# Squared-relu attention and MLP: score tiles leave PSUM through VectorE's relu, with the square on ScalarE

## The chip, the core and the metric

The kernel runs on one core of a Trainium2 chip. A core has TensorE (matrix products into PSUM), VectorE, ScalarE, GpSimd and the DMA queues. The metric is device time in microseconds of one execution.

## What is computed

Attention with a squared relu instead of a softmax, and behind it an MLP with a squared relu:

```python
scores = scale * np.matmul(q, k.transpose(0, 1, 3, 2))   # (8, 12, 448, 448)
attn = np.maximum(scores, 0.0) ** 2 / S                  # S = 448
attn_out = np.matmul(attn, v)                            # (8, 12, 448, 64)
x = attn_out.transpose(0, 2, 1, 3).reshape(3584, 768)
h = x @ w_in                                             # (3584, 2048)
r = np.maximum(h, 0.0)
out = (r * r) @ w_out                                    # (3584, 768), float32
```

All inputs are float32; the kernel multiplies in float16 and sums in float32.

## The kernel before, in words

The eight batches of 12 heads are cut into 24 units of four heads (`n`), three a batch. A unit has seven rounds (`t`), one for each group of 64 keys. `scores` (line 281) makes one round: four small matmuls with 64x64 weights write to a PSUM tile `sp` of two banks (pool `s_p`, two buffers), 128 partitions by 896 columns for one round with all 448 queries. `soft` (line 288) turns it into the float16 tile `at`, and `av` (line 316) multiplies that with V into two `avt` tiles of the PSUM pool `mm_p` (four buffers). At the end of a unit, or of two, copies bring `avt` to SBUF as `xt` (line 329 on ScalarE, line 331 on VectorE). `h_group` makes the hidden layer from `xt` (line 179), squares its relu with `relu2`, and `o_groups` (line 219) makes the output tiles, copied out by ScalarE (line 227) and stored by SP's queue.

There are two ways from scores to `at`. `relu2` (lines 158, 159): ScalarE squares from PSUM, then VectorE masks the square with (score > 0), reading PSUM again. `relu2_wide` (lines 166, 167): ScalarE's relu goes to a float32 tile `rel` in SBUF (pool `rel_p`, four buffers, shared with the output tiles), and VectorE or GpSimd multiplies it by itself.

Batch 0 is written out by hand: in it all five engines take their instructions in program order. Its queries are done in two parts, 256 and 192 wide (`PARTS`), with two rounds in a PSUM tile, so there are 22 tiles `i`, 11 (`NA`) for each part, of 1024 and of 768 columns; tiles 10 and 21 hold one round. In each turn of the loop TensorE makes the scores of tile `i`, then the A·V products of an older tile (`put(i - 2)` in the first part, `put(i - 3)` in the second), in the second part one hidden half-group (`some_h`, six matmuls), and what stands in `beside`: transposes of later units (`turn_pe`, with a copy out of PSUM on VectorE or ScalarE, line 105), loads, casts (line 89). Tiles 5, 8, 12, 15 and 18 are multiplied by GpSimd (`engs`), the others by VectorE. Ahead of the loop GpSimd's queue holds the casts of units 1 and 2, loads of V, and the loads of the first weights (line 127).

Then the main loop runs over pairs of rounds. A turn makes the scores of two rounds, perhaps all A·V products of an older unit in one burst, then `soft` for both, then loads and casts (`upkeep`), and then so much of the queued hidden and output work as keeps the backlog even (`run_some`). In this part only TensorE and SP follow program order; a planner with a cost model orders the instructions of VectorE, ScalarE and GpSimd. In the rest of batch 1 (`n < 2 * NU`) the second tile of a pair goes by `relu2_wide` with GpSimd, all others by `relu2`.

Of the kernel before, what the change touches and what calls it, by code (L numbers as in the profile page):

```python
# [11 lines left out]
AF = mybir.ActivationFunctionType  # L12
# [4 lines left out]
def kernel(  # L17
# [9 lines left out]
    nc = tc.nc  # L27

    B, H, S, D = q.shape
# [8 lines left out]
    NU = 3  # L38
# [5 lines left out]
    SK = 256.0  # L44
# [29 lines left out]
    def load_qk(n, w, eng, gate=None):  # L74
        b, u = divmod(n, NU)
        t = raw_p.tile([P, 2, TJ * D], FP32, name=w + "f", tag=w + "f")
        if gate is not None:
            gate.memset(t[0:1, 0, 0:1], 0.0)
        src = q if w == "q" else k
        eng.dma_start(  # L80
            out=t,
            in_=src[b, 4 * u:4 * u + 4].rearrange(
                "(f e) (p t) d -> (e p) f (t d)", e=2, t=TJ))
        raw[n, w] = t
# [23 lines left out]
    def load_v(b, us):  # L108

        if b not in vst:  # L110
            vst[b] = v_p.tile([P, NU, 2, TJ * D], FP16, name="vs", tag="vs")
        src = v[b].rearrange("(u x) (p t) d -> p u x (t d)", x=4, t=TJ)
        for r in range(2):
            rows = slice(64 * r, 64 * r + 64)
            hs = slice(1, 3) if r else slice(0, 4, 3)
            if isinstance(us, int):
                nc.gpsimd.dma_start(out=vst[b][rows, us], in_=src[:, us, hs])
            else:
                for i, h in enumerate(range(4)[hs]):
                    nc.gpsimd.dma_start(out=vst[b][rows, :, i], in_=src[:, :, h])  # L120
# [36 lines left out]
    def relu2(ps, dst, scale):  # L157
        nc.scalar.activation(out=dst, in_=ps, func=AF.Square, scale=scale)  # L158
        nc.vector.scalar_tensor_tensor(  # L159
            out=dst, in0=ps, scalar=0.0, in1=dst, op0=ALU.is_gt, op1=ALU.mult)  # L160

    def relu2_wide(ps, dst, scale, eng):

        r = rel_p.tile([P, 2, 512], FP32, name="rel", tag="wide")
        r = r[:, :, 0:ps.shape[-1]]
        nc.scalar.activation(out=r, in_=ps, func=AF.Relu, scale=scale)  # L166
        eng.tensor_mul(dst, r, r)  # L167

    def h_group(b, fs, cols):
        pr = b // 2  # L170
# [114 lines left out]
                    skip_group_check=True)  # L285
        return sp

    def soft(sp, width, eng=None):
        at = at_p.tile([P, 2, 512], FP16, name="at", tag="at")
        at = at[:, :, 0:width]  # L290
        if eng is None:
            relu2(sp[:, :, 0:width], at, SK)
        else:
            relu2_wide(sp[:, :, 0:width], at, SK, eng)
        return at

    avs_open: dict = {}

    def av(n, t, cols=WHOLE, copy=None):

        b, u = divmod(n, NU)
        if b not in xts:
            xts[b] = x_p.tile([P, NM, S], FP16, name="xt", tag="xt")
        w = cols.stop - cols.start
        vs = vst[b]
        at0 = w if w < S and u == 1 else 0
        if t == 0:
            avs_open[n] = avs_open[n - 1] if at0 else [
                mm_p.tile([P, 512], FP32, name="avt", tag="mm") for _ in range(2)]
        ap = avs_open[n]  # L310
        at = ats.pop((n, t))
        for e in range(2):
            for c in range(2):
                f = c ^ e
                r = slice(64 * c, 64 * c + 64)
                nc.tensor.matmul(  # L316
                    ap[f][64 * e:64 * e + 64, at0:at0 + w],
                    lhsT=vs[r, u, e ^ c, t * D:(t + 1) * D],
                    rhs=at[r, e, :],
                    start=(t == 0), stop=(t == TJ - 1), skip_group_check=True)  # L320
        if t < TJ - 1 or (w < S and u == 0):
            return
        for f in range(2):
            dst, src = xts[b][:, 2 * u + f, cols], ap[f][:, 0:w]
            if at0:
                dst = xts[b][:, f:f + 3:2, cols]
                src = ap[f][:, 0:2 * w].rearrange("p (u c) -> p u c", c=w)
            if copy is None:
                nc.scalar.activation(out=dst, in_=src, func=AF.Copy, scale=CX)  # L329
            else:  # L330
                copy.tensor_scalar_mul(dst, src, CX)  # L331
# [41 lines left out]
    with tc.manual_schedule():  # L373
        load_qk(0, "k", nc.sync)
        load_qk(0, "q", nc.scalar)
        for n in (1, 2):
            load_qk(n, "k", nc.sync)
            load_qk(n, "q", nc.sync)
        idle = const_p.tile([P, 512], FP16, name="idle", tag="idle")
        nc.vector.memset(idle, 0.0)  # L380
        ident = const_p.tile([P, P], FP16, name="ident", tag="ident")
        make_identity(nc, ident)
        load_v(0, 0)

        warm = mm_p.tile([P, 512], FP32, name="warm", tag="mm")
        for _ in range(12):
            nc.tensor.matmul(warm, lhsT=idle[:, 0:P], rhs=idle, start=True, stop=True)  # L387
        cast_qk(0, "k", dve)
        cast_qk(0, "q", act)
        turn_pe(0, "k", dve)  # L390
        turn_pe(0, "q", dve)
        cast_qk(1, "k", pool)
        load_v(0, 1)
        cast_qk(1, "q", pool)
        load_v(0, 2)
        cast_qk(2, "k", pool)
        load_w1(0)
        cast_qk(2, "q", pool)
        load_w1(1)
        for w in "kq":  # L400
            load_qk(3, w, nc.sync, nc.gpsimd)
        load_w1(2)
        load_w1(3)

        rounds = [divmod(r, TJ) for r in range(STREAM)]
        tiles = [(part, rounds[r:r + 2]) for part in range(2) for r in range(0, STREAM, 2)]
        NA = len(tiles) // 2
        engs = {z: nc.vector for z in range(2 * NA)}
        engs.update({z: nc.gpsimd for z in (5, 8, NA + 1, NA + 4, NA + 7)})
        beside = {  # L410
            1: [(turn_pe, 1, "k", dve)],
            2: [(turn_pe, 1, "q", dve)],
            3: [(turn_pe, 2, "k", dve)],
            4: [(turn_pe, 2, "q", dve)],
            8: [(load_qk, 4, w, nc.sync, nc.gpsimd) for w in "kq"],
            NA + 1: [(cast_qk, 3, "k", pool), (cast_qk, 3, "q", pool)],
            NA + 4: [(load_v, 1, slice(None)), (load_w2, 0, 0), (load_w2, 0, 1)],
            NA + 6: [(turn_pe, 3, "k", dve)],
            NA + 7: [(load_qk, 5, w, nc.sync, nc.gpsimd) for w in "kq"]
            + [(load_w2, 1, 0), (load_w2, 1, 1)],  # L420
            NA + 8: [(turn_pe, 3, "q", act)],
        }
        first_h = deque(z for f in range(0, NF, 2) for z in h_group(0, [f, f + 1], PARTS[0]))
        made: dict = {}

        def put(i):
            part, rs = tiles[i]
            for n, t in rs:
                ats[n, t] = made.pop((part, n, t))
                av(n, t, PARTS[part], nc.vector if part else None)  # L430

        def some_h():
            for _ in range(NM):
                first_h.popleft()[1]()

        for i, (part, rs) in enumerate(tiles):
            cols = PARTS[part]
            w = cols.stop - cols.start
            sp = None
            for j, (n, t) in enumerate(rs):  # L440
                sp = scores(n, t, sp, j * w, cols)
            at = soft(sp, len(rs) * w, engs.get(i))
            for j, (n, t) in enumerate(rs):
                made[part, n, t] = at[:, :, j * w:(j + 1) * w]
            if 2 <= i < NA + 2:
                put(i - 2)
            if i >= NA + 3:
                put(i - 3)
            if i > NA + 1:
                some_h()  # L450
            for fn, *a in beside.get(i, ()):
                fn(*a)
        for i in range(len(tiles) - 3, len(tiles)):
            put(i)
            some_h()
# [3 lines left out]
    for i in range(STREAM // 2, NB):  # L459
        g = []  # L460
        for r in range(max(STREAM, 2 * i), 2 * i + 2):
            n, t = divmod(r, TJ)
            g.append((n, t, scores(n, t)))
        if i in avs:
            for t in range(TJ):
                av(avs[i], t)
        for z, (n, t, sp) in enumerate(g):
            ats[n, t] = soft(sp, S, nc.gpsimd if n < 2 * NU and z == 1 else None)
        if i in pushes:
            push_dense(pushes[i])  # L470
        upkeep(i)
        nxt = min([j for j in pushes if j > i] or [NB + 2])
        run_some(max(0.0, (queued - KEEP) / (nxt - i)))
# [37 lines left out]
```

## Time and profile before

| | |
|---|---|
| median of 8 runs | 418.41 us (417.4 to 418.85) |
| the profiled execution | 417.56 us, its span 415.6 us |
| TensorE busy | 396.3 us, 95% |
| VectorE busy | 246.4 us, 59% |
| ScalarE busy | 257.5 us, 62% |
| GpSimd busy | 98.2 us, 24% |
| VectorE's squares in batch 0 (L167) | 17, 22.8 us |
| ScalarE's relus (L166) | 32, 28.1 us |
| VectorE's masks of scores (L159) | 137, 143.7 us |

In the profile PE is TensorE, PEld its weight loads, DVE VectorE, ACT ScalarE, POOL GpSimd, and SP the queue that issues most DMAs. Times are us from the start of the span. Brackets at the end of a timeline row give the idle time before it and what ended it. `x8` is the number of instructions merged in a row. L167 is line 167. The granted clock of TensorE is given as a fraction of full speed.

### The profile page before, as it was taken

Reading aid. Unit: us, or ns where it says so; the run is one execution under the profiler, and the core shown is the slowest. Engines: PE = TensorE matmul, PEld = TensorE weight load, DVE = VectorE, ACT = ScalarE, POOL = GpSimd, SP = SyncE. Lnnn points to the kernel's source line nnn. Section 1 sums busy time; section 2 is a strip of 40 time slices with the busy share of each in tenths; the row PEclk is TensorE's granted clock in tenths of the full one; section 3 lists DMA queues with packets and bytes.
Section 4 is the critical chain, followed back from the end, with each engine's and each line's share of the span. In section 5 each row is a group of like instructions: output and inputs, shape, how many; then the busy total and the mean of one; then the engine's idle time right before and its main releaser. Section 6 shows DMA issues by size and latency. Waiting matters only on the chain.

```text
span 415.6 us, 8125 instructions
## 1 busy us (share of the span) xinstructions
PE 396.3 (95%) x3368; PEld 211.6 (51%) x3368; DVE 246.4 (59%) x297; ACT 257.5 (62%) x404; POOL 98.2 (24%) x115
## 2 busy tenths in 40 slices
PE   7668899999999999999999999999999999999995
PEld 3445476544445444544455444544455445555562
DVE  2868685369875686486664686486664686142200
ACT  3476398778876676676666676676766676243211
POOL 5559677752302201210112301210100000000000
PEclk9669899999999999999999999999999999999998
DMA  8999999879509933790918833690614010201122
GB/s 278 180 236 177 231 269 184 212 173 294 133 2 159 252 79 94 123 197 17 240 45 158 250 80 93 123 198 18 154 39 95 26 39 0 55 25 38 39 76 76
DMA packets 65445, 53.61 MB, mean 129 GB/s; under 512 B 35841, under 2 KB 62209, under 8 KB 65409
## 3 DMA queue, kind: packets, MB, share of 16 engines
q1 hardware_dynamic: 51152, 40.84, 38.9%
q0 software_dynamic: 13984, 11.80, 19.1%
q8 instruction: 26, 0.43, 0.4%
q10 hardware_dynamic: 272, 0.46, 0.3%
q14 instruction: 11, 0.08, 0.1%
HBM read 45.61 MB, written 11.01 MB: 136 GB/s over the span
## 4 chain that ended last, share of the span: by engine, by line
PE 92%; DVE 4%; ACT 2%; issue 1%; POOL 0%; ACTq 0%; DVEq 0%
PE hps L179 36%; PE ops L219 36%; PE sp L281 10%; PE avt L316 8%; DVE at L167 2%; ACT rel L166 1%; PE tps L103 1%; PE warm L387 1%; DVE at L159 0%; POOL at L167 0%; DVE g L159 0%; DVE kT L105 0%; DVE qT L105 0%; ACT at L158 0%; ACT xt L329 0%
## 5 line engine op out<-in xcount | busy, mean ns | idle before, releaser
L159 DVE SCALAR_TENSOR_TENSOR at<-sp,at 128x896 f16<-128x896 f32 x137 | 143.7, 1086 | 81.1 <-ACT at L158 80.8
L179 PE MATMUL hps<-xt,w 128*128 128x448 f16 (+2 forms) x864 | 159.2, 335 | 0.0
L158 ACT ACTIVATE at<-sp 128x896 f16<-128x896 f32 x137 | 118.9, 915 | 62.0 <-PE sp L281 62.0
L219 PE MATMUL ops<-w,g 128*128 128x384 f16 x896 | 157.1, 326 | 0.0
L219 PEld LDWEIGHTS <-g 128*128 128x128 f16 x896 | 84.3, 98 | 67.9 <-issue 14.2
L179 PEld LDWEIGHTS <-w 128*128 128x128 f16 x864 | 80.3, 99 | 69.2 <-issue 11.5
L159 DVE SCALAR_TENSOR_TENSOR g<-hps,g 128x448 f16<-128x448 f32 (+2 forms) x128 | 76.1, 619 | 46.1 <-ACT g L158 45.7
L158 ACT ACTIVATE g<-hps 128x448 f16<-128x448 f32 (+2 forms) x128 | 68.0, 551 | 31.9 <-PE hps L179 31.0
L281 PE MATMUL sp<-qT,kT 64*64 64x448 f16 (+2 forms) x756 | 53.5, 352 | 5.1 <-DVE qT L105 4.0
L89 POOL CAST ks<-kf 128x896 f16<-128x896 f32 x23 | 22.7, 985 | 127.9 <-DMA kf<-in_k_dram 126.8
L227 ACT ACTIVATE osb<-ops 128x384 f32<-128x384 f32 x56 | 27.8, 496 | 38.4 <-PE ops L219 32.7
L316 PE MATMUL avt<-at,vs 64*64 64x448 f16 (+2 forms) x756 | 42.7, 343 | 6.2 <-DVE xt L331 2.0
L166 ACT ACTIVATE rel<-sp 128x1024 f32<-128x1024 f32 (+4 forms) x32 | 28.1, 895 | 13.6 <-PE sp L281 13.6
L281 PEld LDWEIGHTS <-kT 64*64 64x64 f16 x756 | 17.4, 108 | 33.5 <-issue 30.4
L316 PEld LDWEIGHTS <-vs 64*64 64x64 f16 x756 | 23.5, 111 | 19.4 <-issue 9.9
L120 POOL DMA_DIRECT2D vs<-in_v_dram x28 | 17.5, 633 | 50.9 <-PE avt L316 50.9
L167 POOL TENSOR_TENSOR at<-rel 128x896 f16<-128x896 f32 (+2 forms) x15 | 25.2, 1680 | 13.6 <-ACT rel L166 13.5
L167 DVE TENSOR_TENSOR at<-rel 128x1024 f16<-128x1024 f32 (+3 forms) x17 | 22.8, 1355 | 8.0 <-ACT rel L166 7.9
L329 ACT ACTIVATE xt<-avt 128x448 f16<-128x448 f32 (+2 forms) x46 | 22.4, 549 | 3.0 <-PE avt L316 2.9
L89 POOL CAST qs<-qf 128x896 f16<-128x896 f32 x23 | 22.3, 969 | 6.5 <-DMA qf<-in_q_dram 6.4
L387 PE MATMUL warm<-idle 128*128 128x512 f16 x12 | 5.3, 632 | 1.2 <-DVE idle L380 1.2
L103 PE MATMUL tps<-ident,ks 128*128 128x128 f16 x42 | 4.1, 251 | 1.6 <-DVE g L159 1.6
(23 smaller groups left out, 36.6 us busy)
## 6 DMA issues: line engine op xcount, KB each, us to landing
kf<-in_k_dram SPq DMA_DIRECT2D x24, 448.0 KB, 4.6
qf<-in_q_dram SPq DMA_DIRECT2D x23, 448.0 KB, 5.3
out_dram<-osb SPq DMA_DIRECT2D x50, 192.0 KB, 2.7
vs<-in_v_dram POOLq DMA_DIRECT2D x28, 168.0 KB, 5.5
w<-in_moe_w_in_dram POOLq DMA_DIRECT2D x4, 768.0 KB, 14.7
w<-in_moe_w_out_dram POOLq DMA_DIRECT2D x4, 768.0 KB, 20.3
out_dram<-osb SPq DMA_DIRECT2D x12, 96.0 KB, 2.9
vs<-in_v_dram POOLq DMA_DIRECT2D x6, 112.0 KB, 4.0
```

Source lines behind the costliest of these rows:

```text
L89: op(t.rearrange("p t (f d) -> p f t d", f=2), src.rearrange("p f (t d) -> p f t d", d=D))
L120: nc.gpsimd.dma_start(out=vst[b][rows, :, i], in_=src[:, :, h])
L158: nc.scalar.activation(out=dst, in_=ps, func=AF.Square, scale=scale)
L159: nc.vector.scalar_tensor_tensor(out=dst, in0=ps, scalar=0.0, in1=dst, op0=ALU.is_gt, op1=ALU.mult)
L166: nc.scalar.activation(out=r, in_=ps, func=AF.Relu, scale=scale)
L167: eng.tensor_mul(dst, r, r)
L179: nc.tensor.matmul(cell[0][:, i * w:i * w + w], lhsT=w1[f // 4][:, m, (f % 4) * P:(f % 4 + 1) * P], rhs=xts[b][:, m, cols], start=(m == 0) ...
L219: nc.tensor.matmul(cell[0][:, 0:HALF], lhsT=gt[f][:, tb * P:(tb + 1) * P], rhs=w2[hf][f // 8][:, f % 8, :], start=(f == 0), stop=(f == NF ...
L227: nc.scalar.activation(out=cell[1][:, at:at + HALF], in_=cell[0][:, 0:HALF], func=AF.Copy, scale=CO)
L281: nc.tensor.matmul(sp[64 * c:64 * c + 64, e, at:at + w].rearrange("p (t c) -> p t c", c=TP), lhsT=kT[r, t, 64 * e:64 * e + 64], rhs=qT[r, ...
L316: nc.tensor.matmul(ap[f][64 * e:64 * e + 64, at0:at0 + w], lhsT=vs[r, u, e ^ c, t * D:(t + 1) * D], rhs=at[r, e, :], start=(t == 0), stop= ...
L329: nc.scalar.activation(out=dst, in_=src, func=AF.Copy, scale=CX)
```

## The change

A tile can now take its first step on VectorE: the relu out of PSUM, to float32 in SBUF. ScalarE then squares it from SBUF with the scale. The other form, ScalarE's relu and GpSimd's square, stays for some tiles; the form with a multiplication on VectorE is no longer used. In batch 0 tile 2 joins tiles 5, 8, 12, 15 and 18 on ScalarE and GpSimd; the other 16 go VectorE, then ScalarE. There the second step of a vector tile is held back (`seconds`): it is issued in the next turn of the loop, behind the next tile's first step if that is ScalarE's. In the main loop the first tile of each pair goes VectorE, then ScalarE, to the end; the second goes ScalarE, then GpSimd, in batch 1, and by `relu2` after it. Both first steps are issued ahead of both second steps.

```diff
-    def relu2_wide(ps, dst, scale, eng):
+    def by_sbuf(ps, dst, scale, first):
 
         r = rel_p.tile([P, 2, 512], FP32, name="rel", tag="wide")
         r = r[:, :, 0:ps.shape[-1]]
+        if first is nc.vector:
+            nc.vector.tensor_scalar_max(r, ps, 0.0)
+            return lambda: nc.scalar.activation(out=dst, in_=r, func=AF.Square, scale=scale)
         nc.scalar.activation(out=r, in_=ps, func=AF.Relu, scale=scale)
-        eng.tensor_mul(dst, r, r)
+        return lambda: nc.gpsimd.tensor_mul(dst, r, r)
...
-    def soft(sp, width, eng=None):
+    def soft(sp, width, first=None):
...
-        if eng is None:
+        if first is None:
             relu2(sp[:, :, 0:width], at, SK)
-        else:
-            relu2_wide(sp[:, :, 0:width], at, SK, eng)
-        return at
+            return at, None
+        return at, by_sbuf(sp[:, :, 0:width], at, SK, first)
...
-        engs = {z: nc.vector for z in range(2 * NA)}
-        engs.update({z: nc.gpsimd for z in (5, 8, NA + 1, NA + 4, NA + 7)})
+        firsts = {z: nc.scalar for z in (2, 5, 8, NA + 1, NA + 4, NA + 7)}
...
+        seconds: list = []
...
-            at = soft(sp, len(rs) * w, engs.get(i))
+            first = firsts.get(i, nc.vector)
+            if first is nc.vector and seconds:
+                seconds.pop()()
+            at, second = soft(sp, len(rs) * w, first)
+            if seconds:
+                seconds.pop()()
+            if first is nc.vector:
+                seconds.append(second)
+            else:
+                second()
...
+        seconds.pop()()
         for i in range(len(tiles) - 3, len(tiles)):
             put(i)
             some_h()
...
+        todo = []
         for z, (n, t, sp) in enumerate(g):
-            ats[n, t] = soft(sp, S, nc.gpsimd if n < 2 * NU and z == 1 else None)
+            first = nc.vector if z == 0 else nc.scalar if n < 2 * NU else None
+            ats[n, t], second = soft(sp, S, first)
+            todo.append(second)
+        for second in filter(None, todo):
+            second()
```

## The prediction, made blind

> **What bounds the kernel now.** I read the page first, then the busy time by stretches, then the timeline of the first 60 us. By stretches (us, busy and count of each engine, granted clock, DMA share, GB/s):
>
> ```profile
> 12.00:15.50 3.50, 0.43 (x8) 0.24 (x6) 3.50 (x4) 0.00 (x0) 3.50 (x7) 0.78 0.89 111
> 15.50:20.20 4.70, 4.64 (x66) 3.26 (x66) 3.01 (x5) 2.48 (x3) 0.88 (x2) 0.50 1.17 205
> ...
> 42.60:44.65 2.05, 0.02 (x1) 0.00 (x0) 1.77 (x3) 1.05 (x3) 2.05 (x3) 1.00 1.15 157
> 44.65:48.30 3.65, 3.65 (x31) 1.89 (x34) 1.56 (x3) 0.00 (x0) 1.15 (x2) 0.53 1.18 238
> ...
> 50.30:66.00 15.70, 15.67 (x201) 12.10 (x201) 12.13 (x16) 14.55 (x22) 12.41 (x13) 1.00 1.22 254
> 66.00:90.00 24.00, 23.32 (x231) 12.56 (x228) 11.35 (x13) 18.44 (x29) 17.77 (x16) 1.00 0.92 190
> 90.00:385.00 295.00, 295.00 (x2314) 148.99 (x2311) 189.04 (x231) 192.77 (x309) 36.10 (x44) 1.00 0.48 109
> ```
>
> From 90 to 385 us TensorE is busy all the time at full clock; VectorE and ScalarE are at 64% and 65%. Nothing this change does there can gain. TensorE idles 14 us in the first 90, nearly all of it before 50.3, where batch 0 ends and the saturated part begins; a us won there is a us at the end. Two of the idle spells (3.1 us up to 15.5, 2.05 up to 44.65) are followed by half clock. The timeline shows who was late:
>
> ```profile
> 14.74 1.64 POOL L127 DMA_DIRECT2D w<-in_moe_w_in_dram  x2
> 14.90 0.61 DVE L105 COPY qT<-tps 128x896 f16<-128x896 f16 x1
> 15.56 0.43 PE L281 MATMUL sp<-qT,kT 64*64 64x256 f16 x4 [3.13 <-DVE qT L105]
> ...
> 34.57 2.17 DVE L167 TENSOR_TENSOR at<-rel 128x768 f16<-128x768 f32 x1 [0.26 <-ACT rel L166]
> ...
> 37.27 0.94 DVE L167 TENSOR_TENSOR at<-rel 128x768 f16<-128x768 f32 x1
> 37.40 0.55 PE L103 MATMUL tps<-ident,ks 128*128 128x128 f16 x7 [1.64 <-DVE g L159]
> ...
> 44.05 1.01 DVE L331 TENSOR_SCALAR xt<-avt 128x384 f16<-128x384 f32 x2
> 44.65 0.53 PE L316 MATMUL avt<-at,vs 64*64 64x192 f16 x7 [2.03 <-DVE xt L331]
> ```
>
> Each time TensorE waits for a small VectorE step that stands in the queue behind squares. The same square of 768 columns takes 0.94 us alone and 2.17 beside GpSimd's square and DMA issue.
>
> **Prices of the new operations.** The groups of instructions with shapes kept apart (count, busy us, mean ns, idle before):
>
> ```profile
> L166 ACT ACTIVATE rel<-sp 128x896 f32<-128x896 f32 x10 | 9.1, 913 | 0.0
> ...
> L331 DVE TENSOR_SCALAR xt<-avt 128x384 f16<-128x384 f32 x2 | 1.0, 544 | 0.0
> ...
> L89 ACT CAST qs<-qf 128x896 f16<-128x896 f32 x1 | 0.9, 938 | 2.8 <-DMA qf<-in_q_dram 2.8
> ...
> L331 DVE TENSOR_SCALAR xt<-avt 128x192 f16<-128x192 f32 x2 | 0.6, 353 | 0.0
> ```
>
> VectorE's relu is a one-input operation out of PSUM like L331: 0.995 ns a column and 162 ns fixed, so 1.18 us at 1024 columns, 1.05 at 896, 0.93 at 768. The other end is the mask L159, 1086 ns at 896, so 1.21 at 1024; I take L331, the same kind of operation. ScalarE's square out of SBUF is priced by the cast of line 89: 938 against 913 ns, 25 ns more than out of PSUM: 1.05 at 1024, 0.84 at 768. GpSimd's square has its own row (1.89 at 20.87 us, 1.46 at 768). [...]
>
> **Batch 0.** Before, 17 tiles cost VectorE a square (22.8 us, mean 1.35 with the disturbed ones). Now 16 cost it a relu (7 x 1.18, 7 x 0.93, two short ones: 15.9 us). ScalarE trades 16 relus for 16 squares (+0.4 us). Tile 2 joins the GpSimd tiles. I walk the four queues in program order, each step starting when its engine is free and its inputs are there (0.04 us for a handover).
>
> Start: scores of tile 0 end at 8.93. Relus of tiles 0 and 1 on VectorE last to 11.35, ScalarE's square of tile 0 ends at 11.2, so the first A·V starts as before (11.29). The q copy, which waited behind three squares, now follows its transposes at 12.2 and is done at 12.8 rather than 15.5. That stall goes.
>
> What is late next is tile 2. GpSimd's queue, with the casts and weight loads ahead of it, is busy to 14.74 + 1.64 = 16.38; its square ends at 18.3. Nothing queues behind it on GpSimd until tile 5, but TensorE, in order, does: the A·V of tile 2 comes at 18.35 (17.85 before); TensorE idles from 14.2. The whole gain of the start is lost here, with 0.5 us on top.
>
> Tiles 3 to 12: a vector tile's square queues on ScalarE behind the next scalar tile's relu. Scores of 5 end at 20.3 (18.35 + A·V 0.43 + transposes 0.86 + scores 0.6), relu 5 to 21.3, square 4 to 22.3; GpSimd's square of 5 ends at 23.3, the A·V of 5 starts there (22.81 before). Then ScalarE: relu 8 to 25.5, square 7 +1.0, two copies +1.1, squares 9 and 10 +1.6, which is 29.2; relu 12 from 29.7 to 30.5, square 11 to 31.3, two copies to 32.0. The first hidden group needs those: it ends at 32.2, before at 30.75. So 1.4 us late.
>
> Tiles 13 to 21: VectorE's six squares from 31.04 on took 2.67 + 2.17 + 0.94 + 2.00 + 1.25 = 9.0 us; six relus take 5.6. Of these 3.4 us I lose 0.7 to waits for ScalarE, which has squares and the hidden groups' squares in one queue. The copies at 44.05 come at 42.8 (1.4 - 3.4 + 0.7), and the A·V behind them at 43.4 in place of 44.65. TensorE then idles 0.4 us there, not 2.05, so I expect the half clock of 44.65:48.30 to go: from the A·V to the last hidden group 3.9 us, not 5.7. End of batch 0 at 47.4, not 50.35: -3.0. The same walk of the old kernel gives 49.9, 0.4 early, so I book -2.6.
>
> **After batch 0.** Until 90 us GpSimd keeps the second tile of a turn, and the first goes VectorE, then ScalarE. Both PSUM tiles are free after about 1.1 us instead of 2.0 and 1.8; the one such wait in the trace, 0.6 us at 84.6, goes: -0.5. The new wait: ScalarE's square stands behind VectorE's relu, which can stand behind a mask (0.68), and behind the square queue the hidden groups' squares, for which TensorE waits. At least 0, if those are placed first. At most six turns of (1.05 - 0.91 + 0.68) = 4.9 us, less ScalarE's idle time of 1.15 in 50.3:66, less 2.2 that TensorE can run ahead (two PSUM buffers of 12 matmuls; 21 took about 2.0 us): 1.6. With ScalarE at 93% there I take +1.1. From 90 us on each pair costs ScalarE 25 ns more and VectorE 30 less, hidden by the third of each that is idle; uncovered it would be 1.6 us over 63 turns. The relu buffers, four, are now shared with output tiles to the end: 0 to +1, I take 0.
>
> Sum: -2.6 - 0.5 + 1.1 = -2.0. The profiled execution took 417.56 (span 415.6 and 1.96 around it) and would take 415.6; it lies 0.85 below the median, so against 418.41 I forecast 416.4.
>
> **Rivals.** *Clock (slower).* The idle spell before tile 2 grows to 4.2 us, and behind it TensorE is never busy for long. The walk above has half clock from 17 to 30. The trace needed 4.7 unbroken us to get back (15.50:20.20). [...] Half clock to 34, as TensorE is unbroken again only from 32, makes 48.4, to 45 makes 52.8, 2.9 later than the walk of before: 421.3. It decides from about 37 us on. For it: 2.05 idle us sufficed at 44.65. Against: 1.64 us at 37.40 did not, and the mean clock of 29.4 to 42.6 was 0.94. *Hidden anyway.* The late tile 2 and ScalarE's queue eat all: 418.3. [...] *It doesn't do what it says:* if the relu out of PSUM ran at 1.21 us and GpSimd still disturbed it, VectorE's 3.4 us would shrink to about 1 and the time would be 418.8; the q copies out of PSUM took 0.61 us beside GpSimd too, so I give that little.
>
> **How the numbers follow.** Forecast 0.44 (own range 415.2 to 417.5), more gain 0.13, hidden anyway or undone 0.18, clock 0.25. About 0.2% (0.84 us) is the least that a measurement of this kernel can tell from no change. Faster 0.56, same 0.17, slower 0.27. The range reaches from the gain case to near the clock case: 414.2 to 420.8.
>
> **What would show it.** Relu rows on VectorE near 1.18 and 0.93 us without a spread beside GpSimd, no TensorE wait near 12 to 15 us, one of about 4 us that ends with GpSimd at 18.3, the first hidden group ending near 32, A·V behind the copies near 43.4 with clock 1.00 behind it, the last group of batch 0 at 47 to 48, no wait at 84. It is wrong if half clock lasts past 37 us, if GpSimd comes to tile 2 much sooner or later, or if ScalarE's queue makes TensorE wait between 50 and 66.

## The result, and the profile after

The changed kernel takes 415.48 us (median of 11 runs, 414.98 to 416.77), the kernel before, on the same chip, 418.44 (31 runs, 417.38 to 418.85). The ratio is 0.9936, 95% interval 0.9928 to 0.9945: 2.96 us faster. The profiled execution took 415.35 us with a span of 413.6, which is the span that the sum forecast (415.6 - 2.0).

The groups of the changed kernel by line, shapes apart (count, busy us, mean ns, idle before):

```profile
L167 DVE TENSOR_SCALAR rel<-sp 128x896 f32<-128x896 f32 x74 | 80.5, 1088 | 47.2 <-PE sp L284 44.9 <-POOL at L170 1.4
L168 ACT ACTIVATE at<-rel 128x896 f16<-128x896 f32 x74 | 70.3, 950 | 5.2 <-DVE rel L167 4.2
...
L167 DVE TENSOR_SCALAR rel<-sp 128x1024 f32<-128x1024 f32 x7 | 8.5, 1222 | 3.7 <-PE sp L284 2.6 <-ACT at L168 1.1
L168 ACT ACTIVATE at<-rel 128x1024 f16<-128x1024 f32 x7 | 7.4, 1054 | 4.6 <-DVE rel L167 4.6
L167 DVE TENSOR_SCALAR rel<-sp 128x768 f32<-128x768 f32 x7 | 6.7, 955 | 2.6 <-PE sp L284 1.4 <-ACT at L168 1.1
L168 ACT ACTIVATE at<-rel 128x768 f16<-128x768 f32 x7 | 5.9, 842 | 0.0
```

VectorE's relus of batch 0 cost 1.22 and 0.96 us, where 1.18 and 0.93 were reckoned, and they do not spread. ScalarE's squares are as priced (1.05 and 0.84). The busy time by stretches, in the columns of the prediction's fence:

```profile
12.00:15.50 3.50, 1.48 (x27) 0.89 (x27) 2.92 (x4) 1.32 (x2) 3.50 (x7) 1.00 0.84 105
15.50:20.20 4.70, 1.83 (x23) 1.22 (x26) 0.29 (x1) 0.00 (x0) 2.81 (x3) 0.75 1.18 200
...
42.60:44.65 2.05, 1.62 (x24) 0.91 (x26) 2.05 (x5) 1.88 (x3) 2.05 (x3) 1.00 1.25 182
44.65:48.30 3.65, 3.65 (x46) 2.27 (x46) 1.55 (x4) 1.64 (x3) 2.05 (x4) 1.00 1.21 244
...
50.30:66.00 15.70, 13.98 (x187) 10.84 (x180) 10.06 (x14) 14.32 (x22) 12.45 (x10) 1.00 1.22 249
...
90.00:385.00 295.00, 295.00 (x2317) 148.66 (x2316) 194.23 (x233) 199.46 (x311) 36.09 (x44) 1.00 0.49 109
```

TensorE works more in the first stretch (1.48 us against 0.43), much less in the second (1.83 against 4.64), and the idle spell at 42.60 and the half clock behind it are gone. In 50.30:66.00 it has lost 1.7 us of work. In the last stretch it is as busy as before. The rows of batch 0 on the timeline:

```profile
11.40 0.62 DVE L105 COPY qT<-tps 128x896 f16<-128x896 f16 x1 [0.43 <-PE tps L103]
...
14.76 1.64 POOL L127 DMA_DIRECT2D w<-in_moe_w_in_dram  x2
...
16.40 1.91 POOL L170 TENSOR_TENSOR at<-rel 128x1024 f16<-128x1024 f32 x1
18.37 0.64 PE L318 MATMUL avt<-at,vs 64*64 64x256 f16 x8 [4.80 <-POOL at L170]
...
34.84 1.47 POOL L170 TENSOR_TENSOR at<-rel 128x768 f16<-128x768 f32 x1 [0.94 <-ACT rel L169]
...
35.05 0.96 DVE L167 TENSOR_SCALAR rel<-sp 128x768 f32<-128x768 f32 x1 [0.27 <-PE sp L284]
...
43.39 0.36 PE L318 MATMUL avt<-at,vs 64*64 64x192 f16 x7 [0.32 <-DVE xt L333]
```

The q copy no longer waits behind squares (11.40, not 14.90). Tile 2 makes TensorE wait 4.80 us behind GpSimd's queue. VectorE's relu at 35.05 lies wholly beside a GpSimd square and takes 0.96 us; the square that stood there before took 2.17. The copies' A·V comes at 43.39.

To find where time comes and goes, I took the start of the same matmul in each profile and subtracted its start in the profile of before (us; negative is earlier). The labels of the columns are those of the experiments below.

| matmul (start before) | after | b0_only | main_only | b1_before | no_hold | t2_vector | t2_b1_before | t2_b1_unit5 | before_again |
|---|---|---|---|---|---|---|---|---|---|
| A·V of tile 1 (15.73) | -3.41 | -3.39 | +0.99 | -3.41 | -3.42 | -2.86 | -2.06 | -2.82 | +1.48 |
| A·V of tile 2 (17.64) | +0.73 | +0.52 | +0.98 | +0.67 | +0.91 | -3.69 | -2.34 | -3.65 | +1.48 |
| start of the main loop (50.28) | -2.61 | -1.20 | +1.21 | -2.67 | +0.34 | -7.85 | -5.94 | -7.80 | +1.53 |
| scores (67.43) | -0.78 | -1.20 | +3.03 | -2.67 | +2.17 | -6.02 | -5.94 | -7.80 | +1.53 |
| scores (79.28) | -0.58 | -1.20 | +3.25 | -2.68 | +2.39 | -5.81 | -5.95 | -6.67 | +1.53 |
| scores (89.55) | -0.77 | -0.33 | +2.80 | -2.28 | +1.72 | -4.90 | -5.11 | -6.54 | +1.53 |
| from 126 to the end | -2.07 | -0.33 | +1.50 | -3.59 | +0.42 | -6.20 | -6.41 | -7.84 | +1.52 |

Down the first column: batch 0 gains 2.61 us, batch 1 gives 2.03 of it back, and between 90 and 126 us, where nothing was to be gained, 1.30 come.

### The profile page after: what moved, and what is told of

Read it like the earlier page. It is cut to its first block, busy times and chain, and to the rows that moved or that the text cites. A ratio compares the mean times of both kernels' runs of the same rounds, so it can differ in the third digit from the quotient of the medians.

```text
span 413.6 us, 8059 instructions
## 1 busy us (share of the span) xinstructions
PE 393.4 (95%) x3368; PEld 209.2 (51%) x3368; DVE 244.9 (59%) x296; ACT 264.0 (64%) x404; POOL 97.8 (24%) x116
## 4 chain that ended last, share of the span: by engine, by line
PE 82%; ACT 6%; DMA 3%; POOL 3%; DVE 3%; issue 1%; SPq 1%; ACTq 0%; POOLq 0%; DVEq 0%
PE ops L222 33%; PE hps L182 33%; PE sp L284 8%; PE avt L318 7%; DMA qf<-in_q_dram 3%; ACT at L168 2%; ACT rel L169 2%; POOL at L170 1%; DVE rel L167 1%; ACT g L158 1%; DVE g L159 1%; POOL w L127 1%; PE tps L103 1%; POOL qs L89 0%; SPq L80 0%
## 5 line engine op out<-in xcount | busy, mean ns | idle before, releaser
L167 DVE TENSOR_SCALAR rel<-sp 128x896 f32<-128x896 f32 (+2 forms) x90 | 96.9, 1078 | 54.2 <-PE sp L284 48.9
L158 ACT ACTIVATE at<-sp 128x896 f16<-128x896 f32 x63 | 57.8, 917 | 62.6 <-PE sp L284 62.6
L168 ACT ACTIVATE at<-rel 128x896 f16<-128x896 f32 (+2 forms) x90 | 84.6, 941 | 10.3 <-DVE rel L167 9.4
L158 ACT ACTIVATE g<-hps 128x448 f16<-128x448 f32 (+2 forms) x128 | 66.6, 539 | 20.5 <-PE hps L182 19.1
L159 DVE SCALAR_TENSOR_TENSOR at<-sp,at 128x896 f16<-128x896 f32 x63 | 68.6, 1089 | 3.1 <-ACT at L158 0.9
L89 POOL CAST ks<-kf 128x896 f16<-128x896 f32 x23 | 21.5, 934 | 127.8 <-DMA kf<-in_k_dram 125.2
L170 POOL TENSOR_TENSOR at<-rel 128x896 f16<-128x896 f32 (+2 forms) x16 | 26.8, 1680 | 15.5 <-ACT rel L169 15.4
L169 ACT ACTIVATE rel<-sp 128x896 f32<-128x896 f32 (+2 forms) x16 | 14.7, 916 | 11.5 <-PE sp L284 9.6
L103 PE MATMUL tps<-ident,qs 128*128 128x128 f16 x42 | 3.7, 234 | 1.7 <-DVE g L159 1.7
```

Of the source, the lines that this page charges most:

```text
L89: op(t.rearrange("p t (f d) -> p f t d", f=2), src.rearrange("p f (t d) -> p f t d", d=D))
L159: nc.vector.scalar_tensor_tensor(out=dst, in0=ps, scalar=0.0, in1=dst, op0=ALU.is_gt, op1=ALU.mult)
L167: nc.vector.tensor_scalar_max(r, ps, 0.0)
L168: return lambda: nc.scalar.activation(out=dst, in_=r, func=AF.Square, scale=scale)
L170: return lambda: nc.gpsimd.tensor_mul(dst, r, r)
```

## Experiments

None of them changes what is computed. Each median stands beside the kernel before on the same chip (418.33 us for the first four, 418.25 for the others).

**Each half alone.** b0_only has the new batch 0 and the old forms in the main loop:

```diff
-            first = nc.vector if z == 0 else nc.scalar if n < 2 * NU else None
-            ats[n, t], second = soft(sp, S, first)
-            todo.append(second)
-        for second in filter(None, todo):
-            second()
+            ats[n, t], second = soft(sp, S, nc.scalar if n < 2 * NU and z == 1 else None)
+            if second is not None:
+                second()
```

> Batch 0 as in the changed kernel, main loop as in the old one. If the gain is VectorE's shorter queue in batch 0, the last hidden group of batch 0 ends near 47.7 us and the median is 418.4 - 2.6 = 415.8 (415.3 to 416.3); no TensorE wait behind ScalarE at 54 and 65 us. If the main loop carries the gain and batch 0's is eaten by later waits, 417.5 to 418.4.

main_only has the old batch 0, with ScalarE's relu and VectorE's multiplication, and the new main loop:

```diff
+        if first == "dve2":
+            nc.scalar.activation(out=r, in_=ps, func=AF.Relu, scale=scale)
+            return lambda: nc.vector.tensor_mul(dst, r, r)
...
-        firsts = {z: nc.scalar for z in (2, 5, 8, NA + 1, NA + 4, NA + 7)}
+        firsts = {z: "dve2" for z in range(2 * NA)}
+        firsts.update({z: nc.scalar for z in (5, 8, NA + 1, NA + 4, NA + 7)})
```

> Main loop as in the changed kernel, batch 0 as in the old one. If batch 0 carries the gain: batch 1 gives away up to 2.0 us and the turns after it win 1.6, so 418.4 to 418.9. If the main loop carries the gain: 415.5 to 416.

b0_only took 416.54 us (ratio 0.9964, 0.9952 to 0.9976), main_only 418.52 (1.0008, 1.0002 to 1.0015). b0_only lies above the 415.3 to 416.3 expected of batch 0 alone, main_only within the 418.4 to 418.9 expected if batch 0 carries the gain. They add to -1.6, not to -2.96. The table says why their times alone settle little: b0_only has the same batch 0 as the changed kernel, but the profiled execution, the slowest of its five, was at clock 0.80 between 30 and 45 us, against 0.95, and reached the main loop at -1.20 instead of -2.61. What the table does settle is the stretch from 90 to 126 us. All with the new form in the main loop gain 1.30 us there (main_only 2.80 to 1.50, b1_before 2.28 to 3.59, the changed kernel 0.77 to 2.07); b0_only, with the old form, gains 0.00. The chain of waits of the kernel before in this stretch:

```profile
99.47 0.58 PE sp L281 x8
100.06 1.66 PE avt L316 x28
```

of the changed kernel:

```profile
98.60 0.50 PE sp L284 x8
99.10 1.32 PE avt L318 x28
```

and of b0_only:

```profile
99.14 0.58 PE sp L284 x8
99.72 1.66 PE avt L318 x28
```

The same 28 A·V products take 0.34 us longer in the old form. From 90 to 126 us the old chain has two such bursts and six groups of scores that are 0.08 to 0.16 us over 0.50, 0.11 + 2 x 0.08 + 0.16 + 0.13 + 0.16 = 0.72 and 2 x 0.34: 1.40. The new chain has 2 x 0.05 on other rows. The difference is the 1.30. These are waits which do not show as idle time: TensorE's records run on through them. The timeline of before suggests what the products wait for:

```profile
97.53 2.09 DVE L159 SCALAR_TENSOR_TENSOR at<-sp,at 128x896 f16<-128x896 f32 x2 [0.21 <-ACT at L158]
...
99.86 1.86 PE L316 MATMUL avt<-at,vs 64*64 64x448 f16 x28
...
100.21 1.08 PEld L316 LDWEIGHTS <-vs 64*64 64x64 f16 x26 [0.39 <-issue]
```

In a narrower window, 99.9:100.0, the rows are cut to what overlaps it, so that the first hidden mask and the first product of the burst stand alone:

```profile
99.54 0.61 DVE L159 SCALAR_TENSOR_TENSOR g<-hps,g 128x448 f16<-128x448 f32 x1
99.67 0.38 PE L281 MATMUL sp<-qT,kT 64*64 64x448 f16 x4
...
99.86 0.35 PE L316 MATMUL avt<-at,vs 64*64 64x448 f16 x1
```

The same place in the changed kernel:

```profile
96.12 1.08 DVE L167 TENSOR_SCALAR rel<-sp 128x896 f32<-128x896 f32 x1
...
97.12 1.08 DVE L159 SCALAR_TENSOR_TENSOR at<-sp,at 128x896 f16<-128x896 f32 x1
...
98.12 1.16 DVE L159 SCALAR_TENSOR_TENSOR g<-hps,g 128x448 f16<-128x448 f32 x2
...
98.75 1.25 PEld L318 LDWEIGHTS <-vs 64*64 64x64 f16 x28
...
98.93 1.49 PE L318 MATMUL avt<-at,vs 64*64 64x448 f16 x28
```

A pair costs VectorE about the same (2.09 us in these rows, 1.08 + 1.08 in the new form), but the relu needs no square ahead of it, so VectorE starts sooner and comes sooner to the masks. In the old form the last four of eight score products start at 99.67, behind the mask that reads the score tiles (97.53 + 2.09 = 99.62). Of the burst, one product starts at 99.86; the other 27 follow from 100.20 on, behind the first hidden mask (g), which ends at 99.54 + 0.61 = 100.15 and frees one of the four PSUM tiles that A·V, too, takes its tiles from (pool `mm_p`). The weight loads stop after two for 0.39 us. In the new form the score mask ends at 98.20 and the first hidden mask at 98.73, both before TensorE comes to the scores (98.53) and to the burst (98.93), and the weight loads run through. That the bursts are shorter because of the new main loop is shown by the runs. Which part of it does it, the relu on VectorE or the order that puts both first steps ahead, no run separates; and that the PSUM tile is what the products wait for is read from these rows, and no run tried it alone. Why the old form has no such waits behind 126 us I can't say.

**Batch 1.** b1_before is the changed kernel with the old forms kept in the rest of batch 1:

```diff
-            first = nc.vector if z == 0 else nc.scalar if n < 2 * NU else None
+            if n < 2 * NU:
+                first = nc.scalar if z == 1 else None
+            else:
+                first = nc.vector if z == 0 else None
...
-            todo.append(second)
-        for second in filter(None, todo):
+            if second is not None:
+                second() if n < 2 * NU else todo.append(second)
+        for second in todo:
```

> As the changed kernel, but batch 1 keeps the old forms; from batch 2 on the first tile of a pair goes VectorE, then ScalarE. If batch 1's new form costs 1.7 to 2.0 us between 50 and 72 us and the split of the pair wins 1.3 behind 92 us: 415.5 - 1.7 = 413.8 (413.4 to 414.5). If the waits at 54 and 65 us come from the earlier start of the main loop and not from the form: 415.3 or more.

It took 414.52 us (0.9915, 0.9893 to 0.9937), at the upper end of the 413.4 to 414.5 expected. The interval overlaps that of the changed kernel, so the times alone don't separate them; the profiles do. b1_before keeps its lead of 2.67 to 79 us, and it ends 1.5 us ahead (-3.59 against -2.07). The waits that it lacks, on the timeline of the changed kernel:

```profile
50.13 0.95 ACT L168 ACTIVATE at<-rel 128x896 f16<-128x896 f32 x1 [1.75 <-DVE rel L167]
...
53.73 1.16 DVE L159 SCALAR_TENSOR_TENSOR g<-hps,g 128x512 f16<-128x512 f32 x2 [1.44 <-ACT g L158]
...
54.48 0.55 PE L103 MATMUL tps<-ident,qs 128*128 128x128 f16 x7 [0.92 <-DVE g L159]
...
64.31 0.95 ACT L168 ACTIVATE at<-rel 128x896 f16<-128x896 f32 x1 [0.82 <-DVE rel L167]
...
65.17 0.96 ACT L331 ACTIVATE xt<-avt 128x448 f16<-128x448 f32 x2
...
65.74 0.97 PE L222 MATMUL ops<-w,g 128*128 128x384 f16 x5 [0.80 <-ACT xt L331]
```

At 65.74 TensorE waits for a copy on ScalarE; the copy stands behind ScalarE's square, and the square has just waited 0.82 us for VectorE's relu. At 54.48 it waits for a mask on VectorE, and the mask for the hidden groups' squares on ScalarE; ScalarE had waited 1.75 us for a relu at 50.13 and worked without a break from then on. The lead shrinks by 1.08 us at 54.48 and by 0.96 at 65.74. This is the wait that the prediction added, in the place where it put it.

**Tile 2.** t2_vector gives it back to the vector tiles:

```diff
-        firsts = {z: nc.scalar for z in (2, 5, 8, NA + 1, NA + 4, NA + 7)}
+        firsts = {z: nc.scalar for z in (5, 8, NA + 1, NA + 4, NA + 7)}
```

> As the changed kernel, with tile 2 on VectorE and ScalarE, so that nothing of batch 0 waits for GpSimd's loads. If the idle spell of 4.8 us before tile 2 is on the path, the same walk of the queues ends batch 0 2.9 us sooner: 412.6 (412 to 413.5). If later waits swallow it (GpSimd's square of tile 5, ScalarE's queue), 415 to 415.5.

It took 411.25 us (0.9859, 0.9838 to 0.988), 4.2 less than the changed kernel and below the 412 to 413.5 expected. Two of its five runs took 413.3 and 413.4 us, the other three 411.2. The path of tile 2 on its timeline:

```profile
10.96 1.21 DVE L167 TENSOR_SCALAR rel<-sp 128x1024 f32<-128x1024 f32 x1
...
12.21 1.06 ACT L168 ACTIVATE at<-rel 128x1024 f16<-128x1024 f32 x1 [0.60 <-DVE rel L167]
...
13.95 0.39 PE L318 MATMUL avt<-at,vs 64*64 64x256 f16 x8
```

The square of tile 2 is done at 13.27 and its A·V starts without a wait at 13.95, not at 18.37. At this row the changed kernel is 4.4 us behind it (+0.73 against -3.69), at the main loop 5.2, since its half clock lasts from 17.8 to 31.5 us and that of t2_vector from 18.4 to 25.2, and at the end still 4.1.

**The hold.** no_hold issues a vector tile's square in its own turn, right behind its relu:

```diff
-            if first is nc.vector and seconds:
-                seconds.pop()()
...
-            if seconds:
-                seconds.pop()()
-            if first is nc.vector:
-                seconds.append(second)
-            else:
-                second()
+            second()
...
-        seconds.pop()()
```

> As the changed kernel, but in batch 0 each square is issued at once in its own turn, ahead of the next tile's first step. If the gain is VectorE's queue and the order on ScalarE matters little: 415.5 within 0.8, with the same idle spell of 4.8 us before tile 2. If holding the square back is part of the gain: relus of tiles 2, 5, 8, 12, 15, 18 come up to 1 us later on ScalarE and the score tile is freed later: 416.5 or more.

It took 417.54 us (0.9986, 0.9975 to 0.9997): of the 2.96 us, 2.1 are gone, as expected if holding the square back is part of the gain. Not all of the 2.95 us between the two profiles at the main loop (+0.34 against -2.61) is the hold: the granted clock was 0.80 between 30 and 45 us here and 0.95 in the changed kernel. The fair neighbour is b0_only, with the held order and the same clock (0.50 and 0.50 in the first two stretches, 0.67 from 20.20 to 30.00, 0.80 from 30 to 45; no_hold has 0.51 in the first and the same in the others). It reached the main loop at -1.20, so the hold is worth 1.54 us there. The timeline shows how it is lost:

```profile
36.92 0.96 DVE L167 TENSOR_SCALAR rel<-sp 128x768 f32<-128x768 f32 x1 [0.72 <-PE sp L284]
...
37.91 0.84 ACT L168 ACTIVATE at<-rel 128x768 f16<-128x768 f32 x1 [1.74 <-DVE rel L167]
...
38.66 0.58 ACT L158 ACTIVATE g<-hps 128x512 f16<-128x512 f32 x1
...
39.27 0.69 DVE L159 SCALAR_TENSOR_TENSOR g<-hps,g 128x512 f16<-128x512 f32 x1 [1.40 <-ACT g L158]
39.88 0.95 DVE L167 TENSOR_SCALAR rel<-sp 128x768 f32<-128x768 f32 x1
40.02 0.55 PE L103 MATMUL tps<-ident,ks 128*128 128x128 f16 x7 [1.08 <-DVE g L159]
...
40.86 0.84 ACT L168 ACTIVATE at<-rel 128x768 f16<-128x768 f32 x1 [1.62 <-DVE rel L167]
```

ScalarE idles 1.74 us for VectorE's relu; the hidden group's square (g, 38.66) stands behind it in ScalarE's queue, its mask on VectorE waits 1.40 us for it, and behind the mask stands the next relu, for which ScalarE idles again, 1.62 us. The two engines take turns, and TensorE waits 1.08 us at 40.02. Held back for a turn, the square finds its relu done, and the hidden square comes first: ahead of its squares of 768 columns ScalarE idles 0.0 us in the changed kernel.

**A test of the sum, and the floor of batch 1.** t2_b1_before puts t2_vector and b1_before together, and t2_b1_unit5 besides gives GpSimd no tile in the last unit of batch 1 (`first = nc.scalar if z == 1 and n < 2 * NU - 1 else None`). The reason for the second is this piece of the timeline of b1_before:

```profile
76.64 0.93 POOL L89 CAST ks<-kf 128x896 f16<-128x896 f32 x1 [4.62 <-DMA kf<-in_k_dram]
...
77.53 1.68 POOL L170 TENSOR_TENSOR at<-rel 128x896 f16<-128x896 f32 x1
...
79.24 0.92 ACT L169 ACTIVATE rel<-sp 128x896 f32<-128x896 f32 x1 [1.28 <-POOL at L170]
...
80.21 0.57 PE L284 MATMUL sp<-qT,kT 64*64 64x448 f16 x8 [1.13 <-ACT rel L169]
```

GpSimd's square stands behind a cast that waits 4.62 us for its load; ScalarE's relu then waits for the `rel` buffer, and TensorE for ScalarE.

> Tile 2 on VectorE and ScalarE, batch 1 as in the old kernel, from batch 2 on the new form. If the two gains add (4.2 and 1.0): 410.2. If batch 1 has a floor near 80 us, where TensorE waits for GpSimd's square behind a cast that waits for its load, part of it is lost there: 410.8 to 411.5, with a TensorE wait of 2 us or more at 75 to 80 us.

> As the run before it, but the last unit of batch 1 gives no tile to GpSimd, so no score tile waits behind a cast for units 7 and 8. If GpSimd's queue is the floor at 80 us: 1.5 to 3 us below the run before it, 408 to 409.5. If TensorE waits there for the loads of q and k themselves: no change.

t2_b1_before took 411.20 us (0.9834, 0.9822 to 0.9847), t2_b1_unit5 410.08 (0.9813, 0.9795 to 0.9831). The sum of 410.2 expected for the first was missed: its main loop starts at -5.94, 1.9 later than that of t2_vector with the same batch 0 (the first scores come 0.8 later, and the clock of 12.00:15.50 is 0.79 against 1.00), and TensorE waits 1.58 us at 77.39 for a relu of ScalarE that waits for a `rel` buffer. In t2_b1_unit5 that wait is gone, but two of 0.61 us for VectorE's masks came (66.49 and 76.15). Followed through the table, t2_b1_unit5 is 1.86 us ahead of t2_b1_before where the main loop starts and 1.43 at the end, so between these two profiles the edit itself gains nothing: it loses 0.43, and the lead is the start, where the edit changes nothing. The 1.1 us between the medians fall short of the 1.5 to 3 expected of a floor in GpSimd's queue, and the intervals overlap; what the edit is worth from the same start stays open. It has the lowest median of the study, 5.4 us below the changed kernel.

**How far two executions differ.** before_again is the kernel before, once more:

> The old kernel once more, for a second profile. If its executions differ by how long TensorE runs at half clock in batch 0, the lead of the changed kernel at the first score of the main loop moves by up to 1 us between two profiles while all later steps repeat to 0.1 us.

It took 419.17 us with a span of 417.2. The later steps repeat as expected, but the delay of 1.53 us is more than the 1 us expected, and it is not the half clock: all but 0.05 of it is there at the A·V of tile 1, behind a q copy that comes 1.48 us later (16.38, not 14.90), and from the main loop on it stays within 0.01 us. The row that makes it:

```profile
9.73 4.85 DVE L167 TENSOR_TENSOR at<-rel 128x1024 f16<-128x1024 f32 x2 [1.57 <-ACT rel L166]
```

These are VectorE's squares of tiles 0 and 1. In the first profile of before they took 3.10 us (at 10.01). Here GpSimd's cast of k ran from 7.67 instead of 6.91, since its load came 0.76 us later, and the GpSimd work that followed fell on the squares in another way. So these two executions of the old kernel differ by VectorE's first squares; that GpSimd's casts and loads beside them make the difference is likely from the rows (a square of 768 columns took 0.94 us alone and 2.17 beside GpSimd's in before), but no run tried it. Those of b0_only and of the changed kernel have the same batch 0 without these squares, agree within about 0.2 us up to tile 2, and part later, with the clock of 30 to 45 us (0.80 and 0.95).

## Why the prediction was right, and where it was not

**Batch 0: right, step by step.** The stall behind the q copy is gone and the wait for tile 2 stands in its place (4.80 us from 13.57 on; 4.2 from 14.2 in the walk), GpSimd's square of tile 2 done at 18.31 (18.3 forecast), the A·V of tile 2 at 18.37 (18.35), the first hidden group ending at 32.2 (32.2), the A·V behind the copies at 43.39 (43.4), the last hidden group at 47.74 (47.4). The lead at the main loop is 2.61, booked 2.6. That it agrees to the tenth is in part luck with the clock: the same batch 0 had a lead of 2.67 in b1_before and of 1.20 in b0_only. That the whole gain of the start is lost at tile 2 is shown by t2_vector. The prices held, too: the relus cost 0.03 to 0.04 us more than reckoned. Against the kernel before, the relus cost VectorE at most 15 ns more a tile (0.955 us at 768 columns against 0.94 for the undisturbed square at 37.27 of before, and 1.22 at 1024 against 1.22 for the one at 17.09), and the squares cost ScalarE at most 37 ns more than its relus (950 at 896 columns against 913).

**What carries the gain of batch 0: credited to the wrong part.** The prediction wrote that VectorE's squares "took 2.67 + 2.17 + 0.94 + 2.00 + 1.25 = 9.0 us; six relus take 5.6", as if a shorter VectorE queue were the gain. The queue is as short in no_hold, and there the main loop starts at +0.34, 1.54 us behind b0_only at the same clock. The shorter queue pays only when ScalarE's square does not make the rest of ScalarE's queue wait for the relu. The walk had the held order in it, so its number came out right; the reason given was half of it.

**Batch 1: right in mechanism, short in size.** "With ScalarE at 93% there I take +1.1" against -2.61 to -0.58, 2.03. The bound of at most 1.6 was itself too small: it let TensorE run ahead by 2.2 us, but at 54.48 and 65.74 TensorE stood in order before transposes and an output group, not before scores. One of the prediction's own signs of being wrong came true with it, "if ScalarE's queue makes TensorE wait between 50 and 66", though its sum had booked that wait. The 0.5 us at 84.6 did not come whole: the wait there shrank from 0.61 to 0.18 us and did not go, and the lead grows by only 0.19 from 79 to 90 us. "The relu buffers ... 0 to +1, I take 0" should have been taken at more than 0. VectorE's relu waits 1.41 us for a GpSimd square to give one back (in the first row of the groups above, under POOL), and a relu of ScalarE at 80.70 waits 1.66 us in the same way; behind it TensorE's scores come late at 81.67, and 0.36 us of the lead are lost there.

**After 90 us: wrong.** "From 90 to 385 us TensorE is busy all the time at full clock ... Nothing this change does there can gain." It gained 1.30 us there. A busy share of 100% was taken for work without waits. The chain of waits of before had the evidence: groups of the same eight products at 0.50, 0.58 and 0.66 us, bursts of the same 28 at 1.32 and 1.66.

The three misses in the sum, +0.9 in batch 1, +0.3 at 84 us and -1.3 behind 90, cancel to -0.1; so that the span came out to the tenth is luck in part, besides the clock of batch 0. The sum is now -2.61 + 2.03 - 0.19 - 1.30 = -2.07.

**The last 0.9 us, from the profile to the median.** I added 0.85 us because the profile of before lay that far below its median, and so expected the same of the profile after. But that distance belonged to one execution: before_again lies 1.6 us above it, by two squares that took 4.85 us in place of 3.10, and the changed kernel has no such squares. Its profile (415.35) lies at its median (415.48), so the medians differ by 2.96 where the spans differ by 2.0. Of the 0.96 between, 0.21 lies outside the span (1.96 us around it before, 1.75 after). For the rest, two profiles are no measure of how often the old kernel's squares are so long, so this is a likely cause and not a shown one.

**The rivals.** The clock fell to half behind the wait for tile 2 as feared, but only to 31.5 us, and from then on it was full: in 44.65:48.30 it is 1.00. The gain case at the low end of the range (414.2) counted on full clock throughout batch 0, at 0.7 us. No run shows that term; half clock lasted from 17.8 to 31.5 us here, and from 18.4 to 25.2 in t2_vector, where tile 2 does not wait. In the profile of before it lasted from 13.96 to 20.79, from 24.20 to 31.03 and from 44.68 to 48.09 us: two, two and one steps of 3.41 us. In the changed kernel it is four such steps, from 17.83 to 31.48, and they begin at other places than those of before. Two of these steps in the changed kernel:

```profile
21.24:24.65 3.41, 2.13 (x41) 1.81 (x40) 2.10 (x2) 2.34 (x3) 1.89 (x1) 0.50 1.16 275
...
28.07:31.48 3.41, 3.33 (x48) 2.12 (x41) 2.26 (x3) 2.80 (x5) 0.79 (x1) 0.50 1.24 208
```

and one in b0_only:

```profile
29.07:32.48 3.41, 3.17 (x38) 1.53 (x35) 1.34 (x3) 2.82 (x5) 2.38 (x3) 0.50 1.21 235
```

TensorE was busy for 62%, 98% and 93% of them; the clock stayed at half behind the first, rose to full behind the second, and stayed at half behind the third. Over the first 60 us of the profiles of before and after, taken in such steps, one at half clock was followed by full clock where TensorE was busy for 96% of it or more, and by half at 53 to 84%; one at full clock was followed by half at 0 to 41%, and by full at 52% or more. The same batch 0 kept half clock to 31.5 us in one execution and to 35.9 in another (b0_only), whose steps lay on other gaps. VectorE's relu of 0.96 us beside a GpSimd square (35.05) spoke against the rival that the change doesn't do what it says.

## What to carry to other kernels

When two engines share a step in sequence, each in-order queue should hold other work between the first half and the second; without it a cheaper first half is worth little (2.1 of 2.96 us here by the medians, 1.5 between two profiles with the same clock). Walk the queue of every engine that a moved tile joins: tile 2 behind GpSimd's weight loads cost 4.2 us, more than the change gained. Before two profiles are subtracted, compare the granted clock of each stretch: two executions of the same batch 0 differed by 1.4 us with it. And before an engine at 100% is called a floor, compare equal groups of its instructions with each other: here bursts of the same 28 products took 1.32 and 1.66 us, and the longer ones hid waits.

## What the hardware showed

VectorE's multiplication of two operands in SBUF took 0.94 us alone and 2.17 beside a GpSimd square (before: it began at 34.57, 0.10 us behind GpSimd's, which began at 34.47 and took 1.46), while its relu out of PSUM took 0.95 to 0.96 us in both cases (after), and GpSimd's casts of batch 0 fell from up to 1.66 to 0.95 us. Why they take longer side by side, no run tried.

The old kernel's first two squares took 3.10 us in one execution and 4.85 in the next, where a load came 0.76 us later. That they met GpSimd's work in another way is the likely reason, but no run tried it. So a single profile is compared with another to within some 1.5 us here, unless the same instruction is followed through both.
